# Attention and gated MLP on one core: transposes, high-part products and halves of low-part products of e as separate steps

## Chip, cores and metric

The kernel runs on one core of one Trainium2 chip, as one program. The metric is the device time of one execution in microseconds; the kernel before has a median of 945.14 us over 3 runs.

## What is computed

Eight batches of attention over 8 heads, 576 positions and a head size of 64 with rotated q and k, and behind it a gated MLP that also mixes positions. All of it is float32 in and out.

```python
q_rot, k_rot = (rotate(q), rotate(k))
scores = scale * np.matmul(q_rot, k_rot.transpose(0, 1, 3, 2))
scores = scores - np.max(scores, axis=-1, keepdims=True)
attn = np.exp(scores)
attn = attn / (np.sum(attn, axis=-1, keepdims=True) + 1e-09)
x = np.matmul(attn, v)                      # heads side by side: 512 columns
h = np.maximum(x @ w_in, 0.0)
u, v = (h[..., :512], h[..., 512:])
v_n = (v - mean(v)) / np.sqrt(var(v) + 1e-06)
v_s = np.einsum('ts,bsd->btd', w_spatial, v_n) + b_spatial[None, :, None]
out = (u * v_s) @ w_out
```

## The kernel before

Products of float32 precision are made from two float32r parts of each operand, a high part (rounded) and a low part (the rest): high x high, high x low and low x high are added up in PSUM.

The work goes by pairs of heads: 32 pairs (8 batches of 4). The first four pairs use `attention_plain`; the other 28 use `attention`, which the change touches. A pair has nine tiles of score rows, in three chunks of three tiles (`CHUNKS`). For each tile, `scores` (L574) makes the scores on TensorE (sc), their maximum on VectorE (nmx, L614) and the exponential e on ScalarE (L616). For each chunk, `values` (L618) then does, for each of five blocks of 128 keys (kt = 0 to 4; the last one holds what is left of the keys):

- `transpose` (L628 to L633): three 128x128 blocks of e (for kt = 4 one of 128 and one of 64 columns) are transposed by TensorE into one PSUM tile tp; e is what is loaded into the array, the identity is what streams;
- `high` (L644): ScalarE rounds tp into hi (eh, 384 columns);
- `low` (L357, called in `low`): VectorE takes the rest, lo (el). For kt = 4 there is no lo of its own, both parts share one tile;
- `multiply` (L650 to L657): TensorE multiplies the high and low parts of v (128 columns of weights) with hi, and the high part of v (64 columns of weights) with lo, and adds both to the PSUM tile pv. The first and third chunk have one span of 384 columns (one head); the second chunk has two, of 192 columns each (two heads).

When the fifth block is done, ScalarE copies one half of pv to avt (L674) and VectorE adds the other (L672). `mlp` (L774) makes the MLP of a batch in four stages on TensorE: pa (L804), pb (L827), pc (L845) and pd (L863); it is worked off between the attention of the next batch's pairs.

The order of all this is not written down: `Program.run` (L152) plays the kernel through when it is built, as a list of events. Each step has an engine, a cost in ns and a key; of the steps whose inputs are there and whose buffers are free, an engine takes the one with the lowest key. A step's result is there after its cost and a latency by engine (`LATENCY`: 200 ns for TensorE). The instructions are put out in that order, so each engine's queue is fixed before the launch. Buffers come from pools (`SLOTS`): tp from pm (3 slots, shared with the MLP's sums), pv has 1 slot, hi, lo and avt come from eh (7 slots). For the planner a transpose step is 110 ns for each transpose, and the product step is the sum over its matmuls of `pe_ns`, the larger of loading time and streaming time:

```python
def pe_ns(n, m=P):
    return max(m * 5 // 6 + 3, n * 11 // 24)
```

Of the kernel before, what the change touches and what calls it, by code (L numbers as in the profile page):

```python
# [17 lines left out]
P = 128  # L18
# [6 lines left out]
NQ = 5  # L25
# [3 lines left out]
BACC = {"dynamic_dma_scratch_size": 256}  # L29

PE, ACT, DVE, POOL, DMA = "pe", "act", "dve", "pool", "dma"
LATENCY = {PE: 200, ACT: 142, DVE: 118, POOL: 95, DMA: 1700}
TO_PE = 105
SLOTS = {
# [16 lines left out]
CW = 3 * P  # L51
# [18 lines left out]
S_AT = [-0.24, 4.67, 2.11]  # L70
KT_STEP = 1.19
K_MAX, K_EXP, K_T, K_HI, K_LO, K_AV, K_HALF, K_ADD = 3.66, 16.17, 8.38, -7.48, 1.67, 4.25, 6.99, 12.36
K_LOAD, K_ROPE, K_SUM, K_HIQ, K_LOQ, K_LOK, K_STACK, K_STACK2, K_V, K_VLO = 27, 8, 8, 9, 9, 11, 30, 8, -2, -9
NORM = [-11.45, 57.29, 34.19, 6.63, 21.14]
FIRST = 6
# [9 lines left out]

def pe_ns(n, m=P):
    return max(m * 5 // 6 + 3, n * 11 // 24)


def act_ns(n):  # L90
# [22 lines left out]
class Op:  # L113
    def __init__(self, costs, key, f, new, port, late):
        self.costs, self.key, self.f, self.new, self.port = costs, key, f, new, port
        self.eng, self.late = None, late
        self.waits, self.after, self.bufs = 0, [], []
        self.unknown, self.due = 0, 0


class Program:
# [5 lines left out]
    def op(self, eng, ns, key, f, r=(), w=(), new=(), port=False, late=0):  # L127
        return self.either({eng: ns}, key, lambda e: f(), r, w, new, port, late)
# [23 lines left out]
    def run(self, make, warm):  # L152
        free = {p: list(range(n)) for p, n in SLOTS.items()}
        ready = {e: [] for e in LATENCY}
        soon = {e: set() for e in LATENCY}

        own = dict.fromkeys(SLOTS, 0)
# [4 lines left out]
        def place(bufs):  # L162
# [11 lines left out]
                own[b.pools[0]] -= 1  # L174
            return True

        busy = dict.fromkeys(LATENCY, False)
        held = dict.fromkeys(LATENCY, False)
        events = [(0, n, "ready", o) for n, o in enumerate(self.ops) if not o.waits]
        n, left = len(self.ops), len(self.ops)  # L180
        idle = 0
        events.append((WARM_FROM, n, "wake", None))
        n += 1
        heapq.heapify(events)
        index = {o: k for k, o in enumerate(self.ops)}
        while events:
            now = events[0][0]
            while events and events[0][0] == now:
                _, _, what, o = heapq.heappop(events)
                if what == "ready":  # L190
                    for n_e, e in enumerate(o.costs):
                        heapq.heappush(ready[e], (o.key + STEAL * n_e, index[o], o))
                elif what == "wake":
                    pass
                elif what == "free":
                    busy[o] = held[o] = False
                    if o == PE:
                        idle = now
                        heapq.heappush(events, (now + (WARM_AFTER if now > WARM_FULL else 0), n, "wake", None))
                        n += 1  # L200
                elif what == "place":
                    free[o.pool].append(o.slot)
                else:
                    for b in o.bufs:
                        b.users -= 1
                        if not b.users:
                            late = TO_PE if b.pool in PSUM and o.eng != PE else 0
                            heapq.heappush(events, (now + late, n, "place", b))
                            n += 1
                    for a in o.after:  # L210
                        a.waits -= 1
                        if not a.waits:
                            late = TO_PE if PE in a.costs and o.eng != PE else 0
                            heapq.heappush(events, (now + late, n, "ready", a))
                            n += 1
            for e in LATENCY:
                if busy[e]:
                    continue
                passed, chosen = [], None
                while ready[e] and not chosen:  # L220
                    item = heapq.heappop(ready[e])
                    if item[2].eng:
                        continue
                    other = {DVE: POOL, POOL: DVE}.get(e)
                    if item[2].port and other and held[other]:
                        passed.append(item)
                    elif place(item[2].new):
                        chosen = item[2]
                    else:
                        passed.append(item)  # L230
                if chosen and e in PATIENT:
                    soon[e] = {a for a in soon[e] if not a.eng and a.due > now}
                    if any(a.key < min(chosen.key, UNTIL) and a.due < now + chosen.costs[e] * 0.5 for a in soon[e]):
                        for b in chosen.new:
                            free[b.pool].insert(0, b.slot)
                            own[b.pools[0]] += 1
                        passed.append(item)
                        chosen = None
                for item in passed:
                    heapq.heappush(ready[e], item)  # L240
                if e == PE and not chosen and max(WARM_FROM, idle + (WARM_AFTER if now > WARM_FULL else 0)) <= now < WARM_TO and (free["pv"] or free["pm"]):
                    chosen = warm()
                    pool = "pv" if free["pv"] else "pm"
                    chosen.bufs[0].pool, chosen.bufs[0].slot = pool, free[pool].pop(0)
                    index[chosen] = len(index)
                    left += 1
                if chosen:
                    for b in chosen.new:
                        b.tile = make(b)
                    chosen.eng = e  # L250
                    chosen.f(e)
                    left -= 1
                    for a in chosen.after:
                        a.unknown -= 1
                        a.due = max(a.due, now + chosen.costs[e] + LATENCY[e] + chosen.late)
                        if not a.unknown:
                            for x in a.costs:
                                soon[x].add(a)
                    busy[e], held[e] = True, chosen.port
                    heapq.heappush(events, (now + chosen.costs[e], n, "free", e))  # L260
                    heapq.heappush(events, (now + chosen.costs[e] + LATENCY[e] + chosen.late, n + 1, "done", chosen))
                    n += 2
        assert not left, "instructions wait for each other"
        return now
# [3 lines left out]
def tile_attention_gated_mlp(  # L268
# [11 lines left out]
    nc = tc.nc  # L280
# [337 lines left out]
    def values(i, c, spans, e2, e1, vs, x32, key, before):  # L618
# [4 lines left out]
        for kt in range(NQ):  # L623
# [1 line left out]
            tp = Buf("pm", None, None, f"tp{n}_{kt}")  # L625
            hi = Buf("eh", [P, CW], F32R, f"eh{n}_{kt}")
            lo = Buf("eh", [P, CW], F32R, f"el{n}_{kt}") if kt < 4 else None
            def transpose(kt=kt, tp=tp):  # L628
                blocks = [e2[:, 4 * P:5 * P], e1[:, 4 * P:]]
                if kt < 4:  # L630
                    blocks = [e[:, c0 + kt * P:c0 + kt * P + P] for e, c0 in ((e2, 0), (e2, S + TW), (e1, 0))]
                for m, e in enumerate(blocks):
                    nc.tensor.transpose(out=tp[:e.shape[1], m * P:m * P + P], in_=e, identity=ident)  # L633

            def split(kt=kt, tp=tp, hi=hi, lo=lo):

# [10 lines left out]
                for p, h, l in split():  # L647
                    rest_lo(nc.vector, l, p, h)

            def multiply(kt=kt, hi=hi, lo=lo):  # L650

                todo = [(hi, slice(0, 2))] + ([(lo, slice(0, 1))] if lo else [])
                for n, (part, vp) in enumerate(todo):
                    rows = 64 * (vp.stop - vp.start)
                    for h, c1, c2, _ in spans:
                        last = kt == 4 and n == len(todo) - 1 and c2 == CW
                        nc.tensor.matmul(pv[0:rows, c1:c2], lhsT=vs[:, kt, h, vp, :], rhs=part[:, c1:c2], start=(kt == 0 and n == 0 and c1 == 0), stop=last)  # L657

            passes = [P, 64] if lo else [P]
            ns = sum(pe_ns(c2 - c1, m) for _, c1, c2, _ in spans for m in passes)  # L660
            op(PE, 110 * (3 if lo else 2), at, transpose, r=["ident", (e2, 0), (e2, 1), (e1, 2), *(held if kt else [])], w=[tp], new=[tp])
            op(ACT, act_ns(CW) if lo else 672, at + K_HI, high, r=[tp, *held], w=[(hi, 0), *([n] if kt == 4 else [])], new=[hi])
            op(DVE, dve_ns(CW) if lo else 755, at + K_LO, low, r=[tp, (hi, 0)], w=[lo or (hi, 1)], new=[lo] if lo else [])
            op(PE, ns, at + K_AV, multiply, r=[(vs, 0), (vs, 1), (hi, 0), lo or (hi, 1)], w=[pv], new=[pv] if kt == 0 else [])
        pieces = [(slice(64 * h, 64 * h + 64), slice(at, at + w), slice(c1, c1 + w)) for h, _, _, parts in spans for c1, at, w in parts]
        first = [] if before is None else [(x32, before)]
        new = [x32] if before is None else []
# [361 lines left out]
```

## Time and profile before

| | us |
|---|---|
| Median of 3 runs | 945.14 (944.21 to 947.38) |
| Span of the profiled execution | 943.9 |
| TensorE matmuls busy | 931.7 |
| ScalarE busy | 745.8 |
| VectorE busy | 678.2 |
| GpSimd busy | 568.6 |

The span runs from the first to the last instruction of the profiled execution; the median of the timed runs lies 1.2 us above it. Busy time of TensorE is the time in which at least one matmul is under way. Matmuls overlap, so the duration of one is longer than what it takes of the engine; the distance from one to the next in a row of like matmuls tells the latter. PEld stands for loads of weights into the array, which run beside matmuls. In a timeline, neighbouring instructions of one kind are merged into one row with their count; its length reaches from the start of the first to the end of the last. The granted clock is a share of TensorE's 2.4 GHz.

### The profile page before, as it was taken

Reading aid. Unit: us, or ns where it says so; the run is one execution under the profiler, and the core shown is the slowest. Engines: PE = TensorE matmul, PEld = TensorE weight load, DVE = VectorE, ACT = ScalarE, POOL = GpSimd, SP = SyncE. Lnnn points to the kernel's source line nnn. Section 1 sums busy time; section 2 is a strip of 40 time slices with the busy share of each in tenths; the row PEclk is TensorE's granted clock in tenths of the full one; section 3 lists DMA queues with packets and bytes.
Section 4 is the critical chain, followed back from the end, with each engine's and each line's share of the span. In section 5 each row is a group of like instructions: output and inputs, shape, how many; then the busy total and the mean of one; then the engine's idle time right before and its main releaser. Section 6 shows DMA issues by size and latency. Waiting matters only on the chain.

```text
span 943.9 us, 19676 instructions
## 1 busy us (share of the span) xinstructions
PE 931.7 (99%) x6714; PEld 857.2 (91%) x6714; DVE 678.2 (72%) x1478; ACT 745.8 (79%) x1839; POOL 568.6 (60%) x500
## 2 busy tenths in 40 slices
PE   8999999999999999999999999999999999999998
PEld 4566799998999989999899999999999998999998
DVE  7998887768866687676877668776786768766331
ACT  4898899778987789787987779877898778977452
POOL 6685677654776557585665657656476665653132
PEclk9999999999999999999999999999999999999999
DMA  8887545455434645445445453536543555430101
GB/s 297 256 241 198 170 114 151 111 161 161 100 107 118 172 128 144 106 120 159 127 113 144 128 140 104 146 108 166 146 103 111 129 160 144 104 67 14 64 1 51
DMA packets 57382, 124.65 MB, mean 132 GB/s; under 512 B 13249, under 2 KB 15169, under 8 KB 57282
## 3 DMA queue, kind: packets, MB, share of 16 engines
q1 hardware_dynamic: 56594, 122.73, 47.4%
q8 instruction: 53, 0.87, 0.4%
q10 hardware_dynamic: 688, 0.66, 0.2%
q14 instruction: 47, 0.39, 0.1%
HBM read 66.03 MB, written 9.58 MB: 80 GB/s over the span
## 4 chain that ended last, share of the span: by engine, by line
PE 75%; ACT 11%; DMA 6%; DVE 3%; POOL 2%; SPq 2%; issue 2%; POOLq 0%; DVEq 0%; ACTq 0%
PE pc L845 13%; PE sc L590 13%; PE pv L657 11%; PE pd L863 11%; PE tp L633 11%; PE pb L827 8%; PE pa L804 5%; ACT e L616 3%; DMA st<-in_qk_dram 3%; ACT eh L644 2%; SPq L351 2%; POOL st L452 1%; PE pv L731 1%; ACT avt L674 1%; DMA ks<-st 1%
## 5 line engine op out<-in xcount | busy, mean ns | idle before, releaser
L357 DVE TENSOR_TENSOR el<-tp,eh 128x384 fp32r<-128x384 f32 x336 | 185.7, 555 | 130.9 <-ACT eh L644 122.6
L644 ACT ACTIVATE eh<-tp 128x384 fp32r<-128x384 f32 (+1 forms) x504 | 217.7, 434 | 65.4 <-PE tp L633 58.1
L616 ACT ACTIVATE e<-sc,nmx 128x576 f32<-128x576 f32 x288 | 213.4, 742 | 49.6 <-DVE nmx L614 46.0
L614 DVE TENSOR_REDUCE nmx<-sc 128x1 f32<-128x576 f32 x288 | 214.4, 749 | 21.8 <-PE sc L590 19.1
L452 POOL TENSOR_TENSOR st<-st,tabs 128x576 f32<-128x576 f32 x122 | 172.0, 1436 | 68.2 <-DMA st<-in_qk_dram 39.2
L633 PE MATMUL tp<-ident,e 128*128 128x128 f32 (+1 forms) x1176 | 197.0, 272 | 0.6 <-DVE eh L357 0.2
L633 PEld LDWEIGHTS tp<-ident,e 128*128 128x128 f32 (+1 forms) x1176 | 146.5, 138 | 12.8 <-DVE el L357 1.8
L657 PE MATMUL pv<-eh,vs 128*128 128x384 f32 (+1 forms) x560 | 147.4, 304 | 0.0
L827 PE MATMUL pb<-x,wi 128*128 128x288 f32 x768 | 146.2, 307 | 0.3
L845 PE MATMUL pc<-wsp,vn 128*128 128x288 f32 x768 | 146.0, 306 | 0.0
L863 PE MATMUL pd<-g,wo 128*128 128x288 f32 x744 | 139.0, 305 | 0.0
L590 PE MATMUL sc<-ks,qs 128*128 128x288 f32 x620 | 135.7, 308 | 3.0 <-ACT e L616 1.3
L804 PE MATMUL pa<-wi,x 128*128 128x512 f32 x448 | 132.6, 406 | 0.0
L590 PE MATMUL sc<-lk,qz 128*128 128x288 f32 x558 | 119.6, 296 | 0.0
L827 PEld LDWEIGHTS pb<-x,wi 128*128 128x128 f32 x768 | 113.3, 189 | 5.2 <-DVE el L357 1.5
L845 PEld LDWEIGHTS pc<-wsp,vn 128*128 128x128 f32 x768 | 113.2, 189 | 1.1
L657 PE MATMUL pv<-el,vs 128*64 128x384 f32 (+1 forms) x448 | 113.8, 295 | 0.0
L863 PEld LDWEIGHTS pd<-g,wo 128*128 128x128 f32 x744 | 109.7, 189 | 2.4 <-PE pc L845 0.4
L590 PEld LDWEIGHTS sc<-ks,qs 128*128 128x128 f32 x620 | 98.1, 189 | 12.4 <-ACT e L616 4.3
L657 PEld LDWEIGHTS pv<-eh,vs 128*128 128x128 f32 x560 | 98.4, 188 | 4.3
L357 POOL TENSOR_TENSOR g<-u,g 128x288 fp32r<-128x288 f32 x64 | 51.8, 819 | 69.7 <-ACT g L354 64.4
L590 PEld LDWEIGHTS sc<-lk,qz 128*128 128x128 f32 x558 | 89.1, 188 | 0.0
(172 smaller groups left out, 1428.5 us busy)
## 6 DMA issues: line engine op xcount, KB each, us to landing
st<-in_qk_dram SPq DMA_DIRECT2D x62, 576.0 KB
ks<-st SPq DMA_DIRECT2D x124, 160.0 KB
qs<-st SPq DMA_DIRECT2D x124, 144.0 KB
vr<-in_v_dram SPq DMA_DIRECT2D x32, 320.0 KB
qz<-st SPq DMA_DIRECT2D x62, 144.0 KB
out_dram<-ob SPq DMA_DIRECT2D x31, 288.0 KB
ws<-in_w_spT_dram SPq DMA_DIRECT2D x2, 576.0 KB
tabs<-in_tab_dram ACTq DMA_DIRECT2D x2, 288.0 KB
```

Of the source, the lines that this page charges most:

```text
L357: eng.tensor_tensor(out=lo, in0=src, in1=hi.bitcast(F32), op=ALU.subtract)
L452: f = lambda e: e.tensor_tensor(out=st[j][:, cols], in0=st[j][:, cols], in1=tabs[:, cols], op=ALU.mult)
L590: nc.tensor.matmul(pt[:, c * 512:c * 512 + HALF], lhsT=lhsT, rhs=rhs[:, k0 + c * HALF:k0 + (c + 1) * HALF], start=(n == 0), stop=(n == len ...
L614: op(DVE, 665, key + k_max, lambda: nc.vector.tensor_reduce(out=nmx.tile, in_=tops(), op=ALU.max, axis=AX.XY, negate=True), r=[pt], w=[nmx ...
L616: op(ACT, 730, key + k_exp, lambda: nc.scalar.activation(e[:, e0:e0 + S].rearrange("p (c n) -> p c n", c=2), tops(), AF.Exp, bias=nmx.tile ...
L633: nc.tensor.transpose(out=tp[:e.shape[1], m * P:m * P + P], in_=e, identity=ident)
L644: nc.scalar.activation(h, p, AF.Copy)
L657: nc.tensor.matmul(pv[0:rows, c1:c2], lhsT=vs[:, kt, h, vp, :], rhs=part[:, c1:c2], start=(kt == 0 and n == 0 and c1 == 0), stop=last)
L804: nc.tensor.matmul(pm.tile, lhsT=lhsT, rhs=win[1, d][:, j, :], start=(d == 0 and n == 0), stop=(d == 3 and n == len(todo) - 1))
L827: nc.tensor.matmul(pm[:, :HALF], lhsT=win[0, d][:, i, f * P:(f + 1) * P], rhs=x[d][:, at:at + HALF], start=(d == 0 and n == 0), stop=(d == ...
L845: nc.tensor.matmul(pm[:, :HALF], lhsT=lhsT, rhs=rhs, start=(t == 0 and n == 0), stop=(t == 4 and n == 1))
L863: nc.tensor.matmul(pm[:, :HALF], lhsT=wout[d,][:, i, m * P:(m + 1) * P], rhs=gs[d][:, at:at + HALF], start=(d == 0 and n == 0), stop=(d == ...
```

## The change

A transpose step becomes three (two for kt = 4), one for each transpose. The product step becomes one step for the high-part product and, for kt < 4, two steps for halves of the low-part product of 192 columns each: where the chunk has one span of 384 columns, its one low-part matmul is cut into two; where it has two spans, its two low-part matmuls are the halves. The high-part product no longer reads lo; the halves read it. The first high-part product of a chunk comes before all halves, the last one behind all of them (token `(pv, 0)`); between these the order is free. Key of a half: that of the block plus 7 (`K_REST`), where the product had 4.25 (`K_AV`).

The planner costs a transpose at 56 ns of its own; every TensorE step also has a lead (109 ns, for a half and for the narrow transpose 56 ns), the time that its load takes, of which the tail of the step before it covers a part. A step that waits only for another TensorE step is now released when that one's cost is over, without the latency. A new function `pair` changes the choice on TensorE: if a half was chosen and the step before it was no transpose, a ready transpose goes first, where its key is less than 6 higher; if the step before was a transpose and the choice is no half, a ready half goes first, where its key is less than 30 higher.

```diff
+TURN, REST, OTHER = "turn", "rest", "other"
+TURN_NS, LEAD_NS, REST_LEAD_NS = 56, 109, 56
+K_REST = 7
+NEAR = {TURN: 6, REST: 30}
...
+        self.kind, self.lead, self.tail = OTHER, LEAD_NS, LEAD_NS
...
+        def pair(passed, chosen, item):
+
+            turned = before is not None and before.kind == TURN
+            if chosen.kind == REST and not turned:
+                want = TURN
+            elif turned and chosen.kind != REST:
+                want = REST
+            else:
+                return passed, chosen, item
+            for it in sorted(ready[PE]):
+                o = it[2]
+                if not o.eng and o.kind == want and it[0] < item[0] + NEAR[want]:
+                    for b in chosen.new:
+                        free[b.pool].insert(0, b.slot)
+                        own[b.pools[0]] += 1
+                    if place(o.new):
+                        ready[PE].remove(it)
+                        heapq.heapify(ready[PE])
+                        return [*passed, item], o, it
+                    assert place(chosen.new)
+            return passed, chosen, item
...
+                        for a in before.after:
+                            if PE in a.costs:
+                                a.waits -= 1
+                                if not a.waits:
+                                    heapq.heappush(ready[PE], (a.key, index[a], a))
...
+                        if o.eng == PE and PE in a.costs:
+                            continue
...
+                if e == PE and chosen:
+                    passed, chosen, item = pair(passed, chosen, item)
...
+                    ns = chosen.costs[e]
+                    if e == PE:
+                        if before:
+                            ns += max(0, chosen.lead - before.tail - (now - since))
+                        before, since = chosen, now + ns
...
-                for m, e in enumerate(blocks):
-                    nc.tensor.transpose(out=tp[:e.shape[1], m * P:m * P + P], in_=e, identity=ident)
+                e = blocks[m]
+                nc.tensor.transpose(out=tp[:e.shape[1], m * P:m * P + P], in_=e, identity=ident)
...
-                todo = [(hi, slice(0, 2))] + ([(lo, slice(0, 1))] if lo else [])
-                for n, (part, vp) in enumerate(todo):
-                    rows = 64 * (vp.stop - vp.start)
-                    for h, c1, c2, _ in spans:
-                        last = kt == 4 and n == len(todo) - 1 and c2 == CW
-                        nc.tensor.matmul(pv[0:rows, c1:c2], lhsT=vs[:, kt, h, vp, :], rhs=part[:, c1:c2], start=(kt == 0 and n == 0 and c1 == 0), stop=last)
...
-            op(PE, 110 * (3 if lo else 2), at, transpose, r=["ident", (e2, 0), (e2, 1), (e1, 2), *(held if kt else [])], w=[tp], new=[tp])
+            def multiply(kt=kt, hi=hi):
+
+                for h, c1, c2, _ in spans:
+                    nc.tensor.matmul(pv[:, c1:c2], lhsT=vs[:, kt, h, 0:2, :], rhs=hi[:, c1:c2], start=(kt == 0 and c1 == 0), stop=(kt == 4 and c2 == CW))
+
+            count = 3 if lo else 2
+            for m in range(count):
+                o = op(PE, TURN_NS, at, lambda m=m, turn=turn: turn(m), r=["ident", (e2, 0), (e2, 1), (e1, 2), *(held if kt else [])], w=[tp], new=[] if m else [tp])
+                o.kind, o.tail = TURN, TURN_NS
+                if m and not lo:
+                    o.lead = REST_LEAD_NS
...
-            op(PE, ns, at + K_AV, multiply, r=[(vs, 0), (vs, 1), (hi, 0), lo or (hi, 1)], w=[pv], new=[pv] if kt == 0 else [])
+            ends = kt in (0, NQ - 1)
+            op(PE, sum(pe_ns(c2 - c1) for _, c1, c2, _ in spans), at + K_AV, multiply, r=[(vs, 0), (vs, 1), (hi, 0), *([] if lo else [(hi, 1)]), *([] if ends else [(pv, 0)])], w=[pv, (pv, 0)] if ends else [], new=[pv] if kt == 0 else [])
+            if lo:
+                for h, c1, c2 in [(h, x, y) for h, c1, c2, _ in spans for x, y in ([(c1, c2)] if c2 - c1 < CW else [(c1, c1 + 192), (c1 + 192, c2)])]:
+                    o = op(PE, (c2 - c1) * 11 // 24, at + K_REST, lambda h=h, c1=c1, c2=c2, kt=kt, lo=lo: nc.tensor.matmul(pv[0:64, c1:c2], lhsT=vs[:, kt, h, 0, :], rhs=lo[:, c1:c2], start=False, stop=False), r=[(vs, 0), lo, (pv, 0)])
+                    o.kind, o.lead, o.tail = REST, REST_LEAD_NS, (c2 - c1) * 11 // 24
```

## Rows read from the trace of the kernel before

**Rows 1.** Busy us of each engine in two stretches; PEclk is the granted clock.

```profile
core 0: us, PE busy (x) PEld busy (x) DVE busy (x) ACT busy (x) POOL busy (x), PEclk, DMA share, GB/s
100.00:880.00 780.00, 777.72 (x5701) 741.16 (x5699) 574.28 (x1283) 644.31 (x1600) 488.00 (x415) 1.00 0.47 125
880.00:943.90 63.90, 60.51 (x408) 57.21 (x407) 15.11 (x50) 25.06 (x60) 15.91 (x16) 0.99 0.10 33
```

**Rows 2.** What weight loads waited for: us in total, times, longest us.

```profile
PEld sc L590 <- ACT e L616: 4.3, 8, 1.7
...
PEld tp L633 <- DVE el L357: 1.8, 6, 0.3
PEld pb L827 <- DVE el L357: 1.5, 6, 0.3
```

**Rows 3.** Matmuls by form: count, busy us, mean ns of one, idle before them.

```profile
L633 PE MATMUL tp<-ident,e 128*128 128x128 f32 x1092 | 187.8, 272 | 0.6 <-DVE eh L357 0.2
...
L657 PE MATMUL pv<-eh,vs 128*128 128x384 f32 x280 | 95.5, 341 | 0.0
L657 PE MATMUL pv<-el,vs 128*64 128x384 f32 x224 | 75.6, 338 | 0.0
L657 PE MATMUL pv<-eh,vs 128*128 128x192 f32 x280 | 51.9, 267 | 0.0
L657 PE MATMUL pv<-el,vs 128*64 128x192 f32 x224 | 38.2, 252 | 0.0
...
L633 PE MATMUL tp<-ident,e 128*64 128x128 f32 x84 | 22.8, 272 | 0.0
```

**Rows 4.** Timeline of matmuls from 500 us: start us, length us, instruction, count.

```profile
500.33 0.34 PE L657 MATMUL pv<-eh,vs 128*128 128x384 f32 x1
500.51 0.34 PE L657 MATMUL pv<-el,vs 128*64 128x384 f32 x1
500.68 0.56 PE L845 MATMUL pc<-wsp,vn 128*128 128x288 f32 x3
...
501.61 0.49 PE L633 MATMUL tp<-ident,e 128*128 128x128 f32 x3
...
506.64 0.36 PE L657 MATMUL pv<-eh,vs 128*128 128x192 f32 x2
```

**Rows 5.** Timeline of weight loads from 500 us, same columns.

```profile
500.34 0.13 PEld L657 LDWEIGHTS pv<-el,vs 128*64 128x64 f32 x1
500.51 0.19 PEld L845 LDWEIGHTS pc<-wsp,vn 128*128 128x128 f32 x1
```

**Rows 6.** Weight loads one by one, second chunk of a pair, 509 us.

```profile
509.24 0.19 PEld L657 LDWEIGHTS pv<-eh,vs 128*128 128x128 f32 x1
509.35 0.14 PEld L657 LDWEIGHTS pv<-el,vs 128*64 128x64 f32 x1
509.44 0.13 PEld L657 LDWEIGHTS pv<-el,vs 128*64 128x64 f32 x1
509.52 0.19 PEld L845 LDWEIGHTS pc<-wsp,vn 128*128 128x128 f32 x1
509.63 0.19 PEld L845 LDWEIGHTS pc<-wsp,vn 128*128 128x128 f32 x1
```

**Rows 7.** Weight loads one by one: transposes of a last block (kt = 4), 115 us.

```profile
115.52 0.13 PEld L657 LDWEIGHTS pv<-el,vs 128*64 128x64 f32 x1
...
115.61 0.14 PEld L633 LDWEIGHTS tp<-ident,e 128*128 128x128 f32 x1
115.70 0.11 PEld L633 LDWEIGHTS tp<-ident,e 128*64 128x64 f32 x1
115.81 0.19 PEld L590 LDWEIGHTS sc<-ks,qs 128*128 128x128 f32 x1
115.92 0.19 PEld L590 LDWEIGHTS sc<-ks,qs 128*128 128x128 f32 x1
```

**Rows 8.** Matmul timeline: first and last of 84 wide and narrow transpose pairs.

```profile
108.87 0.38 PE L633 MATMUL tp<-ident,e 128*128 128x128 f32 x2
...
880.72 0.38 PE L633 MATMUL tp<-ident,e 128*128 128x128 f32 x2
```

**Rows 9.** What follows a transpose on ScalarE and VectorE, by form.

```profile
L644 ACT ACTIVATE eh<-tp 128x384 fp32r<-128x384 f32 x336 | 163.3, 489 | 57.6 <-PE tp L633 52.3 <-DVE x L672 1.6 <-PE pd L863 0.9
...
L357 DVE TENSOR_TENSOR el<-tp,eh 128x384 fp32r<-128x384 f32 x336 | 185.7, 555 | 130.9 <-ACT eh L644 122.6 <-PE pv L657 2.1 <-ACT ob L866 0.2
```

**Rows 10.** Timeline of VectorE: the adds that free pv, second chunk.

```profile
514.21 0.78 DVE L672 TENSOR_TENSOR x<-pv,avt 64x192 f32<-64x192 f32 x3 [0.68 <-ACT avt L674]
```

**Rows 11.** Timeline of matmuls: the next chunk's first high-part product.

```profile
515.50 0.34 PE L657 MATMUL pv<-eh,vs 128*128 128x384 f32 x1
```

More of the change, by code (lines that the diff above doesn't have):

```diff
@@ L181, in run @@
         idle = 0
+        before, since = None, 0
         events.append((WARM_FROM, n, "wake", None))
@@ L259, in run @@
                     busy[e], held[e] = True, chosen.port
-                    heapq.heappush(events, (now + chosen.costs[e], n, "free", e))
-                    heapq.heappush(events, (now + chosen.costs[e] + LATENCY[e] + chosen.late, n + 1, "done", chosen))
+                    ns = chosen.costs[e]
[3 more added lines that the diff above has]
+                        before, since = chosen, now + ns
+                    heapq.heappush(events, (now + ns, n, "free", e))
+                    heapq.heappush(events, (now + ns + LATENCY[e] + chosen.late, n + 1, "done", chosen))
                     n += 2
@@ L627, in values, with turn @@
             lo = Buf("eh", [P, CW], F32R, f"el{n}_{kt}") if kt < 4 else None
-            def transpose(kt=kt, tp=tp):
+            def turn(m, kt=kt, tp=tp):
                 blocks = [e2[:, 4 * P:5 * P], e1[:, 4 * P:]]
@@ L648, in low @@
                     rest_lo(nc.vector, l, p, h)
-            def multiply(kt=kt, hi=hi, lo=lo):
-                todo = [(hi, slice(0, 2))] + ([(lo, slice(0, 1))] if lo else [])
-                for n, (part, vp) in enumerate(todo):
-                    rows = 64 * (vp.stop - vp.start)
-                    for h, c1, c2, _ in spans:
-                        last = kt == 4 and n == len(todo) - 1 and c2 == CW
-                        nc.tensor.matmul(pv[0:rows, c1:c2], lhsT=vs[:, kt, h, vp, :], rhs=part[:, c1:c2], start=(kt == 0 and n == 0 and c1 == 0), stop=last)
@@ L659, in values @@
-            passes = [P, 64] if lo else [P]
-            ns = sum(pe_ns(c2 - c1, m) for _, c1, c2, _ in spans for m in passes)
-            op(PE, 110 * (3 if lo else 2), at, transpose, r=["ident", (e2, 0), (e2, 1), (e1, 2), *(held if kt else [])], w=[tp], new=[tp])
+            def multiply(kt=kt, hi=hi):
+                for h, c1, c2, _ in spans:
+                    nc.tensor.matmul(pv[:, c1:c2], lhsT=vs[:, kt, h, 0:2, :], rhs=hi[:, c1:c2], start=(kt == 0 and c1 == 0), stop=(kt == 4 and c2 == CW))
```

## The prediction

> **What bounds the kernel.** I read the stretches first [rows 1]: from 100 to 880 us TensorE's matmuls are busy for 777.72 of 780 us at a granted clock of 1.00 (the 2.4 GHz level), while ScalarE stands at 644 and VectorE at 574. The last transposes run at about 881; what follows is the MLP of batch 7, 60.5 of 63.9 us busy. So from 100 us on the time is the sum of what each matmul takes in TensorE's queue, its slot, plus very few waits. The waits that the weight loads show for results of this stage (on el: 1.8 and 1.5 us; on e: 4.3 us) are small too [rows 2]. An edit that only reorders TensorE's work can therefore pay in two ways: shorter slots, or fewer of these few us.
>
> **How I read a slot.** The durations in the table of forms are latencies, not slots: matmuls overlap. But three transposes in a row span 0.49 us and one lasts 272 ns, so each step is (490 - 272) / 2 = 109 ns [rows 3, 4]. A high and a low product of 384 columns start 0.18 and 0.17 us before their successors: 175 ns each [rows 4]. Where recorded starts run ahead of the array, I use the weight loads: the load for the next matmul begins within 0.01 us of a matmul's start (the low product starts at 500.51, the load behind it at 500.51 [rows 4, 5]), so the distance of two loads is a slot. In a chunk of two spans [rows 6] the loads stand at 509.24, .35, .44, .52, .63: the first high product (192 columns, a 128-column load behind it) takes 110 ns, the second (a 64-column load behind it) 90, a low product with another behind it 80 to 90, and the last low product, with a 128-column load of another step behind it, 110. So 192 columns stream in about 88 ns, and a 128-column load of float32r data lengthens that to about 110. That price is real, and the change moves it about.
>
> **The transposes, the point that decides.** The planner's new figures (56 ns for a transpose, 109 for the load ahead of one, 56 for a half's load) take a transpose to be 56 ns of streaming that waits for 109 ns of loading. Three readings speak against it. First, the transpose followed by the narrow one (64 columns of weights, half the load): loads at 115.61, 115.70, 115.81 and 115.92 give 90 for the low product ahead, 110 for the transpose, 110 for the narrow one [rows 7]; the first and the last of the 84 such pairs both span 0.38 us, 380 - 272 = 108 [rows 8]. Half the load behind it, and the transpose still takes 109. Second, the same rows have a 192-column low product followed by a transpose: 90 ns, not 110, so a transpose's own load needs no more than 90; it cannot be what makes the next step 109. Third, a transpose lasts 272 ns, a 192-column product 252 and a 384-column one 338 [rows 3]; by that slope (86 ns for 192 columns) 128 columns would be near 223, and 272 fits some 237 columns. I conclude that the transpose of float32 data itself occupies the array for 109 ns, whatever is behind it. A low-part half behind it hides its 64-column load, which was hidden before as well, and saves nothing on the transpose.
>
> The Trainium skill, TensorE: Matmul & The Clock Gate, sections Back-to-back issue gap and LDWEIGHTS, says otherwise: 128 columns stream in about 56 ns at the full clock and a load takes its columns divided by 1.2 GHz, 107 ns for 128 and 53 for 64. By that rule a transpose would be bound by the load behind it and the interleaving would pay. The rows do not agree: 109 ns with either load [rows 4, 7, 8].
>
> **Part by part.** *Three steps in place of one.* The same 1092 + 84 transposes at 109 ns, the same queue: 0 ns. The first still takes the pm slot and the last frees the evacuation; with a half between them a group of three lasts some 180 ns longer, which only pm's holding time pays.
>
> *The low product of 384 columns becomes two of 192.* 224 of them [rows 3], so 224 more matmuls and loads. Each half takes 90 with a transpose behind it, 110 with a 128-column load behind it. Against 175: both before a transpose, +5 ns; both before a wide load, +45. *Chunks of two spans.* 112 steps took 110 + 90 + 85 + about 106 (the last mostly 110 [rows 6], 90 where a transpose follows [rows 7]) = 391. Their high products now lose the low ones behind them, so the second rises from 90 to 110 unless a transpose follows. Best: 110 + 90 + 90 + 90 = 380 (-11); worst: 110 + 110 + 110 + 110 = 440 (+49).
>
> So all halves ahead of transposes: 224 x 5 - 112 x 11 ns = 0 us; none: 224 x 45 + 112 x 49 = +15.6 us. Which share? A chunk has 14 transposes in groups of 3, 3, 3, 3, 2 and 8 halves. A group of three takes a half behind its first and second, and then the next transpose, which carries the lowest key, follows; a third half, or one where a score step has come ready meanwhile, meets a wide load. I take three in four ahead of a transpose: a half costs 0.75 x 90 + 0.25 x 110 = 95; the 384 case +15 x 224 = +3.4 us; the two-span case 110 + 107 + 190 = 407, +16 x 112 = +1.8 us. Together **+5.2 us**.
>
> *Waits.* The high product no longer waits for el; each half does, and behind a half on TensorE's queue stands everything. A half is released by ScalarE's copy (489 ns) and VectorE's subtraction (555 ns) after the transposes [rows 9], and is planned behind a later transpose, so el is normally done. The last high product waits for all eight halves, but that is TensorE's own order. The planner now also releases a TensorE step right behind another one, 200 ns earlier than before, and believes a pair to be shorter than it is: the other engines will be ahead of the plan. From both sides: at best the named waits go (1.8 + 1.5 + 4.3 = 7.6 us [rows 2], some of it ahead of 100 us: -6); at worst they double, +6. I take -1, as this stretch hardly waits.
>
> Sum against the span: 943.9 + 5.2 - 1 = 948.1; the median of the runs stands 1.2 above the span, so **949.3 us**.
>
> **Rivals.** *Faster: the transpose is 57 ns where a half follows.* Then a pair costs 57 (86 / 192 x 128) + 90 = 147, or 57 + 110 if its own load binds, against 109 + 87.5 now; 672 halves x 30 to 49 ns is 20 to 33 us, a time of 912 to 925, say 919. For it: no transpose of before has a float32r half behind it, so the very pair is not in the trace. Against it: the 109 with a narrow load behind. It decides with the first such pair. Chance 0.12.
>
> *No difference.* Nearly every half stands ahead of a transpose and the waits shrink a little: 945, between 942.3 and 948. For it: the next transpose is ready at once. Chance 0.17.
>
> *Faster by waits alone.* Finer steps and accumulators that are finished without a break let most of the waits [rows 2] go while the slots cost little: 936 to 942, say 940. Against it: there is hardly more than that to win. Chance 0.08.
>
> *Slower through pv.* There is one pv slot. A chunk holds it from its first high product (506.64) to the end of its adds (514.99), and the next begins at 515.50: it stands empty for 0.5 to 1.0 us of about 9 [rows 4, 10, 11]. The halves' key is 2.75 later than the product's was; if they come over 1 us later there, the last high product, the copy and the add move out, and every further 0.2 us is 17 us over 84 chunks; with the pairing failing widely (the +15.6 end), 958 to 975, say 963. Against it: TensorE is never without other work and takes overdue keys first. Chance 0.08.
>
> *The forecast*, slots as above: 946 to 957, 0.55.
>
> **Chances and range.** About 0.3% (2.8 us) is what a measurement tells from no change: below 942.3 is faster, above 948.0 slower. Faster: 0.12 + 0.08 = 0.20. Same: 0.17 and the lower fifth of the forecast, 0.12: 0.29. Slower: 0.43 + 0.08 = 0.51. The range of 8 in 10 leaves out the load rival (0.12) and the far parts of the pv and wait rivals (0.08): 938 to 959. The forecast's own is 946 to 957.
>
> **What would show it.** Right: in the changed trace a load of el that begins with a transpose's start is followed by the next load about 0.11 us later (the transpose's slot), and that by the next after 0.09 (the half's); transposes still last 272; TensorE is as busy from 100 to 880 and that stretch grows by some 5 us, evenly over the batches. Wrong: a distance of 0.06 between those loads (the load rival: each batch would shrink by some 3 to 5 us); or slots as said, but idle time on TensorE before hi or el, and pv adds further apart than 9.4 us.

## The result and the profile after

The changed kernel takes 952.55 us (median of 7 runs) where the kernel before, on the same chip, takes 946.14: a ratio of 1.007, with an interval of 1.0052 to 1.0088, so 5 to 8 us slower. The profiled execution spans 950.2 us against 943.9.

TensorE is as full as it was. Busy us by stretch, same columns as [rows 1]:

```profile
core 0: us, PE busy (x) PEld busy (x) DVE busy (x) ACT busy (x) POOL busy (x), PEclk, DMA share, GB/s
100.00:880.00 780.00, 779.37 (x5896) 751.48 (x5894) 569.21 (x1272) 640.16 (x1594) 488.28 (x415) 1.00 0.47 125
880.00:950.20 70.20, 66.84 (x468) 64.05 (x467) 17.37 (x59) 28.26 (x69) 15.99 (x16) 1.00 0.10 37
```

From 100 to 880 us TensorE sits idle for 0.6 us instead of 2.3 and runs 195 more matmuls (the cut adds 224 to the kernel), and 60 more than before are still left behind 880 us (468 against 408). So this stretch did not lose time by idling; what its slots take is read below. The waits for el are now named at three lines (before: [rows 2]):

```profile
PEld pc L894 <- DVE el L401: 0.5, 1, 0.5
PEld tp L678 <- DVE el L401: 0.3, 2, 0.2
PEld pb L876 <- DVE el L401: 0.2, 1, 0.2
```

The matmuls of the changed steps by form (count, busy us, mean ns; before: [rows 3]):

```profile
L678 PE MATMUL tp<-ident,e 128*128 128x128 f32 x1092 | 216.6, 273 | 0.2
L712 PE MATMUL pv<-el,vs 128*64 128x192 f32 x672 | 164.4, 329 | 0.0
...
L698 PE MATMUL pv<-eh,vs 128*128 128x384 f32 x280 | 95.3, 344 | 0.0
L698 PE MATMUL pv<-eh,vs 128*128 128x192 f32 x280 | 52.2, 270 | 0.0
```

A half of 192 columns is recorded with 329 ns, where one not behind a transpose lasted 252 [rows 3]. It is recorded as starting early and then stands some 80 ns behind the transpose that streams. What a slot is shows in the loads, one by one, at the end of a chunk (before: [rows 7]):

```profile
503.26 0.14 PEld L678 LDWEIGHTS tp<-ident,e 128*128 128x128 f32 x1
503.40 0.13 PEld L712 LDWEIGHTS pv<-el,vs 128*64 128x64 f32 x1
503.50 0.11 PEld L678 LDWEIGHTS tp<-ident,e 128*64 128x64 f32 x1
503.59 0.14 PEld L712 LDWEIGHTS pv<-el,vs 128*64 128x64 f32 x1
503.70 0.19 PEld L894 LDWEIGHTS pc<-wsp,vn 128*128 128x128 f32 x1
```

From the load of el at 503.40, which begins with the transpose's start, to the next at 503.50: the transpose takes about 0.11 us (108 ns before the rounding) with a half behind it. From 503.50 to 503.59: the half takes 0.09. From 503.59 to 503.70: the narrow transpose takes 0.11.

Where the time came from, by landmarks. The first MLP product (pa) of batches 1 and 6, before and then after:

```profile
214.38 0.39 PE L804 MATMUL pa<-wi,x 128*128 128x512 f32 x1
778.45 0.39 PE L804 MATMUL pa<-wi,x 128*128 128x512 f32 x1
```

```profile
217.46 0.63 PE L853 MATMUL pa<-wi,x 128*128 128x512 f32 x2
784.09 0.48 PE L853 MATMUL pa<-wi,x 128*128 128x512 f32 x1
```

Five batches took 564.1 and take 566.6 us: 0.5 us more for each on the mean (nothing for the first of the five, 0.5 to 0.8 for the others). But 3.1 us were lost by the time batch 1 began. The transposes of this stage (count, min/median/max ns, first and last start in us) tell where, before and then after:

```profile
L633 PE MATMUL tp<-ident,e x1176: 270/272/332, 99.7 to 880.8; 128*128 128x128 f32 x196
```

```profile
L678 PE MATMUL tp<-ident,e x1176: 270/272/333, 105.3 to 887.8; 128*128 128x128 f32 x196
```

The first comes 5.6 us later, although next to all that runs ahead of it belongs to the first four pairs, whose own steps the change doesn't edit; half of that is made up within the first batch.

### The profile page after: what moved, and what is told of

Its sections match the earlier page's. It is cut to its first block, busy times and chain, and to the rows that moved or that the text cites. A ratio compares the mean times of both kernels' runs of the same rounds, so it can differ in the third digit from the quotient of the medians.

```text
span 950.2 us, 20090 instructions
## 1 busy us (share of the span) xinstructions
PE 936.3 (99%) x6937; PEld 871.9 (92%) x6937; DVE 674.4 (71%) x1474; ACT 745.0 (78%) x1843; POOL 569.2 (60%) x500
## 4 chain that ended last, share of the span: by engine, by line
PE 88%; ACT 5%; DMA 3%; DVE 1%; SPq 1%; issue 1%; ACTq 0%; DVEq 0%
PE sc L634 15%; PE tp L678 13%; PE pc L894 13%; PE pd L912 11%; PE pa L853 10%; PE pb L876 10%; PE pv L698 8%; PE pv L712 6%; ACT e L660 2%; DMA qs<-st 1%; SPq L395 1%; PE pv L780 1%; ACT eh L689 1%; DMA ks<-st 1%; DMA st<-in_qk_dram 1%
## 5 line engine op out<-in xcount | busy, mean ns | idle before, releaser
L401 DVE TENSOR_TENSOR el<-tp,eh 128x384 fp32r<-128x384 f32 x336 | 186.0, 554 | 112.8 <-ACT eh L689 102.4
L678 PE MATMUL tp<-ident,e 128*128 128x128 f32 (+1 forms) x1176 | 233.5, 273 | 0.2
L712 PE MATMUL pv<-el,vs 128*64 128x192 f32 x672 | 164.4, 329 | 0.0
L678 PEld LDWEIGHTS tp<-ident,e 128*128 128x128 f32 (+1 forms) x1176 | 154.6, 138 | 8.5 <-ACT vv L953 1.1
L894 PE MATMUL pc<-wsp,vn 128*128 128x288 f32 x768 | 134.4, 299 | 0.3 <-DVE el L401 0.3
L876 PE MATMUL pb<-x,wi 128*128 128x288 f32 x768 | 131.0, 302 | 0.0
L853 PE MATMUL pa<-wi,x 128*128 128x512 f32 x448 | 129.9, 403 | 0.0
L912 PE MATMUL pd<-g,wo 128*128 128x288 f32 x744 | 124.2, 299 | 0.0
L876 PEld LDWEIGHTS pb<-x,wi 128*128 128x128 f32 x768 | 109.2, 189 | 0.9 <-DVE el L401 0.2
L912 PEld LDWEIGHTS pd<-g,wo 128*128 128x128 f32 x744 | 105.6, 189 | 0.6
L712 PEld LDWEIGHTS pv<-el,vs 128*64 128x64 f32 x672 | 91.2, 137 | 4.4
```

The source lines that it names most:

```text
L401: eng.tensor_tensor(out=lo, in0=src, in1=hi.bitcast(F32), op=ALU.subtract)
L712: o = op(PE, (c2 - c1) * 11 // 24, at + K_REST, lambda h=h, c1=c1, c2=c2, kt=kt, lo=lo: nc.tensor.matmul(pv[0:64, c1:c2], lhsT=vs[:, kt, h ...
L853: nc.tensor.matmul(pm.tile, lhsT=lhsT, rhs=win[1, d][:, j, :], start=(d == 0 and n == 0), stop=(d == 3 and n == len(todo) - 1))
L876: nc.tensor.matmul(pm[:, :HALF], lhsT=win[0, d][:, i, f * P:(f + 1) * P], rhs=x[d][:, at:at + HALF], start=(d == 0 and n == 0), stop=(d == ...
L894: nc.tensor.matmul(pm[:, :HALF], lhsT=lhsT, rhs=rhs, start=(t == 0 and n == 0), stop=(t == 4 and n == 1))
L912: nc.tensor.matmul(pm[:, :HALF], lhsT=wout[d,][:, i, m * P:(m + 1) * P], rhs=gs[d][:, at:at + HALF], start=(d == 0 and n == 0), stop=(d == ...
```

## The experiments

Two ways of reading each profile serve for all of them. *Batches*: the distance of the pa starts of batches 1 and 6. *Waits*: over the loads from 110 to 875 us, I added up what a distance between two loads exceeds the median of its kind of neighbours by, where that is over 40 ns. The kernel before has 6.6 us of it, the changed one 4.5. The sum depends on how neighbours are grouped: by the matmul's form and the next load it comes to 9.2 and 7.0 us. Distances from the kernel before, which are what is used, move by up to 1.5 us with it.

### Is the transpose 109 ns because it streams float32?

In the changed kernel, e is written as float32r and the transposes become float32r products with the identity:

```diff
-                nc.tensor.transpose(out=tp[:e.shape[1], m * P:m * P + P], in_=e, identity=ident)
+                nc.tensor.matmul(tp[:e.shape[1], m * P:m * P + P], lhsT=e, rhs=ident, start=True, stop=True)
```

> The changed kernel with e rounded to float32r as the exponential writes it, and the transposes as float32r products with the identity (the low part of e is then zero: the low bits of e are left out; no step is). Theory (the 109 ns are the streaming of float32): a transpose with a half behind it takes about 57 ns, the half ahead of a transpose becomes load-bound at 110 instead of 90; a pair 167 instead of 199, some 630 pairs, about 20 us faster than the changed kernel: 0.98 to 0.99 of before. A transpose lasts about 223 ns instead of 272. Rival (109 ns come from something that transposes of either type share): slots and time as the changed kernel, 1.007.

Measured: 933.18 us, a ratio of 0.9882 (0.9824 to 0.9939). Matmuls by form:

```profile
L681 PE MATMUL tp<-ident,e 128*128 128x128 f32 x1092 | 190.4, 249 | 0.9 <-ACT vv L956 0.5 <-ACT vv L953 0.2
...
L715 PE MATMUL pv<-el,vs 128*64 128x192 f32 x672 | 132.5, 253 | 0.0
...
L681 PE MATMUL tp<-ident,e 128*64 128x128 f32 x84 | 18.7, 223 | 0.0
```

The narrow transpose falls from 272 to the expected 223, and the half is back at 253: it no longer waits for a transpose that is still streaming. Loads one by one:

```profile
461.33 0.14 PEld L715 LDWEIGHTS pv<-el,vs 128*64 128x64 f32 x1
461.39 0.19 PEld L681 LDWEIGHTS tp<-ident,e 128*128 128x128 f32 x1
461.50 0.14 PEld L715 LDWEIGHTS pv<-el,vs 128*64 128x64 f32 x1
461.57 0.19 PEld L856 LDWEIGHTS pa<-wi,x 128*128 128x128 f32 x1
```

A transpose with a half behind it now takes 0.06 us (461.33 to 461.39, 461.50 to 461.57), and the half ahead of a transpose 0.11, bound by that one's load. A pair is 0.17 instead of 0.20 us. Five batches take 551.5 us (226.72 to 778.24) instead of 566.6: 3.0 us a batch, 21 us over seven, as expected; by the two ratios it is 18, within their intervals. In this trace the first transpose comes only at 116.5, because TensorE's granted clock is 0.50 (the 1.2 GHz level) from 10 to 30 us, where it is busy throughout; from 0 to 10 us, busy for 7.4 us, it is 0.99, and from 110 to 875 us 1.00. The profiled execution took 943.34 us, the three others 931.45 to 933.45, so the median holds none of this. So the planner's figures, 56 for a transpose and 109 for the load ahead of one, come near a float32r transpose. This kernel's are float32.

The replacement swaps two things, the type and the instruction (a transpose becomes a product), and no run parts them. The kernel before has rows that do: in the first four pairs some scores are float32 products of 288 columns, with 64 rows of weights and a 128-column load behind them, at a granted clock of 1.00:

```profile
15.99 1.37 PE L600 MATMUL sc<-kf,st 64*128 64x288 f32 x5
```

One of them lasts 402 ns, so each steps by (1370 - 402) / 4 = 242 ns, 0.84 ns a column. Float32r products of 288 columns step by 133 (three in 0.56 us [rows 4]), 0.46 a column. The transpose's 109 ns are 0.85 a column, so float32 nearly doubles the streaming of a product as well.

The kernel before with the same replacement:

> The kernel before with the same rounding of e and the same float32r products in place of the transposes (the low bits of e are left out). Theory: a transpose followed by a 128-column load stays at 109 ns, now bound by that load; one followed by the narrow transpose falls to about 57, 84 x 52 ns = 4.4 us; a 192-column product ahead of a transpose rises from 90 to 110, 23 times: 0.995 to 0.998 of before. Rival: no slot changes, within 0.2%. With the run of the changed kernel: if that gains some 20 us and this only 4, the interleaving is worth what the planner's figures say only for float32r transposes.

Measured: 943.67 us, 0.9978 (0.9963 to 0.9993). Here 1092 transposes last 256 ns on the mean and the 84 narrow ones 224. A wide transpose ahead of a narrow one falls to 59 ns, but three in a row still step by 110, now bound by the load. Without halves between them, shorter streaming is worth 2 us; with them, 21.

### What does the cut of the low-part product cost?

In the kernel before, alone and in place:

```diff
-                        nc.tensor.matmul(pv[0:rows, c1:c2], ...)
+                        for x, y in ([(c1, c1 + 192), (c1 + 192, c2)] if n and c2 - c1 == CW else [(c1, c2)]):
+                            nc.tensor.matmul(pv[0:rows, x:y], ...)
```

> The kernel before, its steps and its order as they are, with the one low-part matmul of 384 columns put out as two of 192 next to each other. Theory: the first half takes 88 ns, the second 110 ahead of a wide load and 90 ahead of a transpose (about one in five), 194 against 175: 224 x 19 ns = +4.3 us, 1.004 to 1.005 of before. Rival (the added 64-column load is hidden, so a cut costs nothing): within 0.1% of before.

Measured: 948.04 us, 1.0033 (1.0022 to 1.0044), +3 us; five batches 566.3 us (214.07 to 780.40), as long as in the changed kernel. Counted in the loads, 326 of 652 halves have another half behind them (88 ns), 69 a transpose (89), 257 a wide load (109): for the former 384 columns that is 193 against 175, +4.0 us over 224. The waits fell from 6.6 to 4.9. The time is a little below the theory's range, which the interval reaches; the rival falls. The cut is not free, and its price is the wide load behind 192 columns.

In the changed kernel, the product left whole:

```diff
-                for h, c1, c2 in [... for x, y in ([(c1, c2)] if c2 - c1 < CW else [(c1, c1 + 192), (c1 + 192, c2)])]:
+                for h, c1, c2 in [... for x, y in [(c1, c2)]]:
```

> The changed kernel with the low-part product of 384 columns left whole (one step behind a transpose, cost 176 in the plan). Theory (a transpose takes 109 ns whatever is behind it; a half costs 90 ahead of a transpose and 110 ahead of a wide load, 97 on average, so two halves 194 against 175): 224 x 19 ns = 4.3 us faster than the changed kernel, batches near 112.5 us, 1.001 to 1.004 of before. Rival (a transpose is shorter where a half is behind it): fewer places behind transposes are filled, so no faster than the changed kernel, 1.007 or more.

Measured: 951.12 us, 1.0058 (1.0042 to 1.0073). Five batches take 564.65 us (217.78 to 782.43), 2.0 less than in the changed kernel, some 2.8 over seven; against the 4.3 expected, part went into transposes that stand ahead of a product whose el isn't there yet (the slot of the narrow transpose rose to 117 on the mean from 113). In the batches the direction is the theory's. The total decides nothing: its interval overlaps that of the changed kernel and takes in the rival's 1.007. I expected 1.004 at most, from a gain of 4.3 us that came out as 1 to 3.

### What is the pairing worth?

```diff
-                if e == PE and chosen:
-                    passed, chosen, item = pair(passed, chosen, item)
...
-K_REST = 7
+K_REST = 4.25
```

> The changed kernel without the pairing (the choice is by key alone), halves at key +4.25 as the product had. Theory: transposes stand together at 109 each; halves stand next to each other (88) or ahead of wide loads (110), 198 against 175 and in two-span chunks 18 ns more: about 7 us over before in the slots and 2 to 3 in the start, 1.008 to 1.012 of before, so the pairing itself is worth 1 to 3 us. Rival (a half behind a transpose saves 30 to 50 ns): 20 us slower than the changed kernel, 1.025 or more.

Measured: 956.3 us, 1.011 (1.0078 to 1.0143), the slower side of the theory and far from the rival's 1.025. But not for the theory's reason: halves cost 95.4 ns on the mean, less than the 98.0 of the changed kernel, because 312 of them stand ahead of another half. The waits went from 4.5 to 14.4 us. TensorE's busy time from 110 to 875 us points the same way, here without the pairing and then in the changed kernel:

```profile
110.00:875.00 765.00, 761.86 (x5735) 724.74 (x5733) 556.70 (x1249) 621.20 (x1555) 481.75 (x407) 1.00 0.47 125
```

```profile
110.00:875.00 765.00, 764.37 (x5785) 738.22 (x5783) 559.95 (x1256) 629.61 (x1567) 481.02 (x410) 1.00 0.47 125
```

In the slots, pairing costs 1 to 2 us; what it gave is an order with fewer waits. The run changes the halves' key together with the pairing, so the order is the work of both.

### Do the wrong figures in the plan matter?

```diff
-TURN_NS, LEAD_NS, REST_LEAD_NS = 56, 109, 56
+TURN_NS, LEAD_NS, REST_LEAD_NS = 109, 109, 56
...
-                o.kind, o.tail = TURN, TURN_NS
-                if m and not lo:
-                    o.lead = REST_LEAD_NS
+                o.kind, o.lead = TURN, 90
```

> The changed kernel with the slots of the trace in the plan: a transpose 109 ns, the load ahead of one 90. Theory (TensorE is the bound and its order hardly depends on these figures, because pairing is forced): the same slots, 1.005 to 1.008 of before, like the changed kernel. Rival (the optimistic figures spoil the order of the other engines): the waits shrink, 1.003 or less.

Measured: 955.2 us, 1.0098 (1.0066 to 1.013): not better than the changed kernel, so the rival falls; the median is above the theory's range, the interval overlaps it. The waits are 8.4 us. Here, true figures alone did not make a better order.

### Where do the 3 us ahead of batch 1 come from?

The change has a part that touches every TensorE step: one that waits only for another is released when that one's cost is over, 200 ns earlier. Alone, in the kernel before:

```diff
                     if o == PE:
                         idle = now
+                        for a in ran.after:
+                            if PE in a.costs:
+                                a.waits -= 1
+                                if not a.waits:
+                                    heapq.heappush(ready[PE], (a.key, index[a], a))
...
                     for a in o.after:
+                        if o.eng == PE and PE in a.costs:
+                            continue
```

> The kernel before with one thing of the change: the planner releases a TensorE step right behind another TensorE step, 200 ns earlier. Theory (the stretch ahead of the first chunk of pair 4 grew from 99.7 to 105.3 us because this rule reorders the first four pairs): the first transpose of pair 4 comes at 103 to 106 us, by batch 1 some 3 us are left, the batches keep 112.6 us; time 1.002 to 1.005 of before. Rival (the longer start comes from the new steps and their pairing): first transpose near 100 us, time within 0.2% of before.

Measured: 952.7 us, 1.0077 (1.0061 to 1.0093), as slow as the whole change. The first transpose comes at 103.9 us, and the batches run from 217.38 to 783.34, 566.0 us:

```profile
L643 PE MATMUL tp<-ident,e x1176: 269/272/332, 103.9 to 886.6; 128*128 128x128 f32 x196
```

The start is as the theory said. The batches are not: they are 0.4 us longer each, by waits (11.6 us; TensorE's busy time from 110 to 875 us is 761.1 us against 764.0). In the changed kernel from which this release is taken away, except between transposes:

> The changed kernel without that release, except from one transpose to the next. Theory: the start is as before (first transpose of pair 4 near 100 us), the batches stay at 113.1 us, so 3 of the 6.3 us go: 1.003 to 1.005 of before. Rival (the start is lengthened by the new steps): as the changed kernel, 1.007.

Measured: 962.49 us, 1.0174 (1.0155 to 1.0193). The first transpose is back at 100.0, and everything behind it is worse: TensorE is busy for 759.6 of 765 us, and the waits are 15.5 us. Both expectations fall for the total. In these kernels early release hurts the old steps and helps the new ones, so it can't be judged by taking it out everywhere. The next runs switch it by the time of the plan: up to 100 us late, then early. In the changed kernel:

```diff
-                            if PE in a.costs:
+                            if PE in a.costs and (before.quick or a.kind == before.kind == TURN):
                                 a.waits -= 1
...
-                        if o.eng == PE and PE in a.costs:
+                        if o.eng == PE and PE in a.costs and (o.quick or a.kind == o.kind == TURN):
```

with `before.quick = now > 100000`.

> The changed kernel, but up to 100 us of the plan a TensorE step is released by another one as before (200 ns after its end; from transpose to transpose at once). Theory (the early release costs some 3 us ahead of pair 4 and nothing behind it in this kernel): pair 4 starts as before, batches 113.1 us, 1.003 to 1.005 of before. Rival (the rule's price at the start is paid back by the order that it makes there, or the start is lengthened by something else): 1.006 or more.

Measured: 949.81 us, 1.0042 (1.003 to 1.0054). The first transpose comes at 100.0, and five batches (215.56 to 781.93) take 566.4 us, as in the changed kernel. The theory holds and the rival falls. So of the 6.6 us, some 2 to 2.6 are the early release ahead of pair 4: 1.9 by the start of batch 1 (215.56 against 217.46), 2.6 by the ratios. The same in the kernel before:

> The kernel before with the early release from 100 us of the plan on, no other edit. Theory (with the early release alone each batch was 0.5 us longer through waits, whatever the start was): start as before, batches 113.0 us, +3.5 us, 1.003 to 1.005 of before. Rival (the longer batches came from the other order at the start): batches 112.6 us, within 0.2% of before.

Measured: 948.53 us, 1.0031 (1.0019 to 1.0043), five batches 565.9 us (213.48 to 779.40): the longer batches come from the release itself, whatever the start. Both prices together, in the changed kernel with the release from 100 us on and the whole product:

> The same with the low-part product of 384 columns left whole. Theory (start and cut are the two prices of the change and add up): start as before, batches 112.8 us, within 0.2% of before, 1.000 to 1.003. Rival (they do not add, because each new order brings waits of its own): 1.004 or more.

Measured: 948.9 us, 1.0034 (1.0017 to 1.0051). This doesn't decide: the interval reaches from the theory into the rival, single runs lie between 946.6 and 952.4, and the profiled one is the slowest of them, with the first transpose at 104.6 (the granted clock of that trace is 0.68 from 30 to 40 us and 1.00 from 110 us on). From batch 2 on its batches take 112.9 us each, close to the theory's 112.8.

### A version that uses the measured slots

The one saving that the rows do show is 20 ns where a transpose comes next behind 192 columns instead of a wide load. In the kernel before, behind a two-span product, a ready transpose goes first:

```diff
+                if e == PE and chosen and chosen.kind != "turn" and ran is not None and ran.kind == "narrow":
+                    for it in sorted(ready[PE]):
+                        o = it[2]
+                        if not o.eng and o.kind == "turn" and it[0] < item[0] + 6:
...
+            o.kind = "narrow" if len(spans) > 1 else None
```

> The kernel before with one preference on TensorE: behind a two-span product step, whose last low-part product of 192 columns costs 110 ns ahead of a 128-column load and 90 ahead of a transpose, a ready transpose step goes next if its key is less than 6 higher. In the emitted order 76 of 113 such steps are followed by a transpose instead of 23. Theory: 53 x 20 ns = 1.1 us less in the slots, waits unchanged: 0.998 to 1.000 of before. Rival (any new order loses some waits' worth of time): 1.001 to 1.005.

Measured: 948.85 us, 1.0032 (1.0009 to 1.0056). The slots came as expected (73 halves at 89 ns ahead of a transpose, before 22; mean of a half 95.5 against 105.8, in which some waits are), but the waits rose from 6.6 to 11.9 us. No version faster than the kernel before, with the same arithmetic, was found.

## Why the prediction was right

**The bound.** TensorE stayed full, and the time grew with its slots: as said.

**The transposes.** They kept 109 ns with a half behind them, now seen in the pair itself, and the float32r run shows the reason that [rows 3, 7, 8] gave: it is the streaming of float32, since the same place falls to 0.06 us with float32r, and float32 products step at the same 0.84 ns a column. The load rival was a true description of another kernel. The Trainium skill's page TensorE: Matmul & The Clock Gate (Back-to-back issue gap, its formula for a matmul by itself, and LDWEIGHTS) comes near the float32r runs: about 56 ns for 128 columns and 107 for a wide load, against 59 to 62 and 109 there.

**The halves.** 90 ahead of a transpose, 110 ahead of a wide load, as worked out from [rows 6, 7]. The share was off: of 650 halves in the loads from 110 to 875 us, 387 stand ahead of a transpose (60%, I took 75), 243 ahead of a wide load, 20 ahead of another half. That makes 97 ns instead of 95: 224 x 19 ns = 4.3 us for the cut product. The two-span high products rose from 102.1 to 106.5 ns on the mean, 280 x 4.4 = 1.2 us (78 of 138 pairs of them now have a wide load behind, before 25), and the 384-column ones from 174 to 176, 0.6 us. Together 6.1 us against the 5.2 of the sum.

**The waits.** I took -1 in a range of -6 to +6; measured over the loads it is -2.1. Slots and waits give +4.0 against some 0.51 x 7 = 3.6 us that the batches show. That this is so close to the forecast's +4.2 is in part luck: the slots came out 0.9 us dearer, the waits 1.1 us cheaper.

**The start.** This term is missing from the sum. I named the early release of TensorE steps only as a cause of fewer waits and looked for its effect where the new steps are. It reorders the first four pairs too, and costs 2 to 2.6 us there, as the run that keeps it out of the first 100 us shows. With it the total is 6 to 7 us. The forecast of 949.3 was 3.3 us short of the median: 1.0 of that is the kernel before itself, whose median is 946.14 over seven runs and was 945.14 over three; the other 2.2 are this term. So the sign "evenly over the batches" held only for the part that the slots make, and the range took in the measured time because it was wide, not because the start was foreseen.

**The pv rival** did not come: pv's 84 stays last 8.5 us on the mean against 8.6, and its adds end 9.4 us apart against 9.3.

**What stays open** is why one order waits 5 us and another 12. The runs name who is waited for in single places, but not a rule. The early release alone lengthens the old steps' batches and shortens the new ones'; that was measured, not explained. Nor is it shown that the prices of the start and of the cut add up.

## What to carry to other kernels

Before filling a gap on TensorE, settle from the trace whether a short matmul is bound by its own streaming or by the next load: one place where a narrower load follows, and its slot, decides it, and the type of the data can change the answer. Cutting a matmul so that it streams for less time than a 128-column load takes cost the difference here wherever such a load followed: 109 ns where 192 columns stream in 88. In an order made by a planner, every edit also changes the waits; here that was worth -2 to +9 us, more than most of these edits moved in the slots, so a rule that touches all steps is to be priced over the whole kernel, the start included.

## What the runs showed of the hardware

A float32 transpose of 128 columns takes 109 ns of TensorE and lasts 272; the same as a float32r product takes 0.06 us and lasts 223 with a narrow load behind it. Float32 products of 288 columns step by 242 ns where float32r ones step by 133. The load of a transpose is quicker than that of a product: ahead of a transpose a 192-column half takes 0.09 us, ahead of its float32r product 0.11, and the load's own record is 0.14 us against 0.19. That is the instruction and not the type: for 64 columns the load's record is 0.11 us for the narrow transpose and 0.14 for the halves and also for float32 products of the first four pairs. And a matmul behind a float32 transpose can be recorded as starting some 80 ns before it streams, so that the mean duration of a form (329 against 252 ns) tells what stands ahead of it.
